# A decode kernel's tail: the last PSUM copy and the output's issue move to ScalarE, and the early zeros with them

## The chip, the cores and the metric

The kernel runs on one core of a Trainium2 chip. A core has five engines that run side by side and meet at semaphores: TensorE (PE, matrix products into PSUM; its weight loads are listed as PEld), VectorE (DVE), ScalarE (ACT), GpSimd (POOL) and SyncE (SP), which here only issues DMAs and waits. DMAs of all issuers run on the core's 16 DMA engines. The metric is the time of one execution on the device in microseconds (us); a profile of one execution gives the single instructions.

## The reference

A decode step of a gated mix of two branches, for a batch of 2 and one token of width 640, all in fp32:

```
g = sigmoid(sum(x * gate_w))
q = (x @ wq) as 32 heads of 128
o = softmax(q . k_cache / sqrt(128)) @ v_cache      # 4096 cached positions per head
a = o (4096 wide) @ wo                              # back to 640
b = silu(x @ w1) @ w2                               # 640 -> 1728 -> 640
out = g * a + (1 - g) * b                           # (2, 1, 640)
```

Nearly all of the work is reading: the two caches are 2 x 32 x 4096 x 128 floats each, 134 MB apiece, and `wq` and `wo` are 10.5 MB each.

## The kernel before, in words

The kernel is written as a list of operations per engine (`Flow`). Each operation names the buffers that it reads and writes; `plan` (line 75) works out from the order in the text which semaphores it must wait for. A write waits for all earlier readers of the same name, and a DMA counts as done once its own semaphore stands at 16. What an engine has already learned through another engine's wait isn't waited for again. Each engine runs its operations strictly in the order of the text.

Three slabs `v`, `b` and `a` of SBUF take the loads, all issued by SP in one order: `w1`, then `x` and the gate, `w2`, `wq` (lines 303 to 312), a DMA of zeros from the cleared buffer `oP` into the output (line 328), and then the caches. There are N = 16 rounds, one for each group of four heads and each row of the batch. A round loads a K part (8.4 MB) and a V part (8.4 MB). DVE and POOL multiply K with the query (lines 670 and 676), DVE sums to scores (686), ACT takes the exponentials (715), PE multiplies them with V (766), and DVE turns the result into columns of `oP` (837). `load_k(i + 2)` waits for the scores of round i, `load_v(i)` for PE's products of round i - 1. Six loads of `wo` follow the last V.

The start: DVE transposes `x` and the gate (line 420), copies `x` into the cleared buffer `xz` (424), works out `x @ w1` (443 to 446), PE the rest of the feed-forward branch (533) and `x @ wq` into two PSUM banks (608). `ps_0` holds heads for u = 0, `ps_1` for u = 1; ACT takes both out into `qall`, once for each row of the batch, four instructions (647). The first K load waits for line 446, since it overwrites `w1`; the first V load waits for line 608.

The end: `in_halves` (556) sums `wo` products for three quarters of the heads into the PSUM bank `early`, `merge` copies that to SBUF on ACT (568) and joins it by matmuls with the sums `acc` in `ps_0` (573), and `in_quarters` (586) adds the last quarter as its pieces of `wo` land. Then DVE copies `acc` to SBUF (891), SP issues the output (892), counts `s_sent` so that POOL may clear the semaphores (904 and 905), and waits for the output to land (897).

`once` (line 123) wraps a stretch of an engine's operations, given by their indices in `spans`, in a loop that runs once, with a hint for fetching code ahead.

## Time and profile before

| | |
|---|---|
| median of 3 runs | 695.96 us |
| lowest and highest | 695.74, 696.21 us |
| the profiled execution | 695.71 us |
| its span, first to last instruction | 694.2 us |
| instructions | 3593 |
| DVE busy | 507.5 us, 73% |
| POOL busy | 265.6 us, 38% |
| PE busy | 211.4 us, 30% |
| ACT busy | 40.0 us, 6% |
| read from HBM | 298.26 MB, 430 GB/s over the span |

A profile row reads: start and length in us (or, for groups, their sum and the mean in ns), engine, line of the kernel, operation, the buffer written and those read, shapes. "SPq" is SP's own instruction stream. In brackets, or behind the bar, stands how long the engine had been idle and what ended that. DMA instructions in such rows are only the issue; the data move later.

### The profile page before, as it was taken

The numbers are of one execution on the slowest core, as the hardware profiler recorded it, in microseconds if no ns is written. First come the engines' busy times: TensorE is split into PE (matmuls) and PEld (weight loads), VectorE is DVE, ScalarE is ACT, GpSimd is POOL, SyncE is SP. The second block draws the span as 40 slices with busy tenths as digits, with TensorE's granted clock in tenths as the row PEclk, the third lists the DMA queues.
The fourth block names the chain that finished last, engine by engine and source line by source line (L and its number), as shares of the span: only waits on it lengthen the run. The fifth ranks groups of instructions, "written<-read, shape, count | busy, mean of one in ns | idle before, by whom it ended". The sixth has DMA issues, their size and how long they took to land. (4 is left out here: it accounts for less than half of the span.)

```text
span 694.2 us, 3593 instructions
## 1 busy us (share of the span) xinstructions
PE 211.4 (30%) x1440; PEld 72.5 (10%) x1440; DVE 507.5 (73%) x269; ACT 40.0 (6%) x152; POOL 265.6 (38%) x26
## 2 busy tenths in 40 slices
PE   0074032151331405060412306060503315050657
PEld 0032010010110101020100101010100101010113
DVE  3810958898989596886959596986959595977811
ACT  0001010101010101010010101010000101010000
POOL 1000808191726090815335180906244270907100
PEclk9998556565565757575665757575655757575689
DMA  9999999999999999999999999999999999999997
GB/s 383 430 446 450 430 427 424 423 457 438 427 430 423 430 461 427 434 423 423 438 457 427 430 423 427 464 430 430 423 423 461 434 430 427 423 438 457 427 408 326
DMA packets 6209, 298.33 MB, mean 430 GB/s; under 512 B 672, under 2 KB 700, under 8 KB 956
## 3 DMA queue, kind: packets, MB, share of 16 engines
q1 hardware_dynamic: 6204, 298.27, 99.4%
q8 instruction: 2, 0.03, 0.0%
q14 instruction: 3, 0.02, 0.0%
HBM read 298.26 MB, written 0.01 MB: 430 GB/s over the span
## 5 line engine op out<-in xcount | busy, mean ns | idle before, releaser
L670 POOL TENSOR_TENSOR slabs<-slabs,qsb 128x7680 f32<-128x7680 f32 x16 | 262.3, 16396 | 378.7 <-DMA slabs<-in_A_k_cache_dram 347.8
L686 DVE TENSOR_REDUCE s<-slabs 128x68 f32<-128x8704 f32 (+1 forms) x32 | 276.3, 8676 | 0.0
L766 PE MATMUL ps<-slabs,pz 128*32 128x512 f32 x1024 | 146.2, 735 | 345.2 <-PEq L145 338.2
L676 DVE TENSOR_TENSOR slabs<-slabs,ps 128x8704 f32<-128x8704 f32 x16 | 147.5, 9218 | 108.5 <-DMA slabs<-in_A_k_cache_dram 108.4
L766 PEld LDWEIGHTS ps<-slabs,pz 128*32 128x32 f32 x1024 | 39.5, 132 | 438.6 <-issue 431.6
L715 ACT ACTIVATE pz<-s,nb 32x128 f32<-32x128 f32 x64 | 25.4, 398 | 556.5 <-PE ps L766 363.2
L804 PE MATMUL ps<-osb,pick 128*128 128x512 f32 x32 | 20.4, 724 | 58.9 <-PEq L145 58.0
L818 DVE TENSOR_REDUCE row<-ps 64x128 f32<-64x512 f32 x16 | 10.9, 682 | 23.3 <-PE ps L804 23.3
L788 DVE SCALAR_TENSOR_TENSOR osb<-ps,rg,own 128x512 f32<-128x512 f32 x16 | 12.0, 748 | 21.4 <-PE ps L766 21.2
L618 PE MATMUL ps<-qall,spread 128*128 (+1 forms) x32 | 7.4, 319 | 35.3 <-PEq L145 34.5
L446 DVE SCALAR_TENSOR_TENSOR slabs<-slabs 128x1728 f32<-128x1728 f32 x8 | 16.1, 2019 | 0.3
L458 PE MATMUL ps<-slabs,xz_col 128*32 128x432 f32 x16 | 3.1, 928 | 33.2 <-DVE slabs L446 33.2
L804 PEld LDWEIGHTS ps<-osb,pick 128*128 128x128 f32 x32 | 5.4, 211 | 73.0 <-issue 71.2
L715 ACT ACTIVATION_READ_ACCUMULATOR pz<-s,nb 32x1 f32 x64 | 11.8, 184 | 0.0
L618 PEld LDWEIGHTS ps<-qall,spread 128*128 128x128 f32 x32 | 6.9, 224 | 44.9 <-issue 43.2
L533 PE MATMUL ps<-slabs,seq 128*32 128x320 f32 x54 | 10.3, 545 | 3.7 <-DVE seq L512 3.7
L825 DVE STREAM_TRANSPOSE ps<-row 64x256 f32<-64x256 f32 x16 | 10.3, 642 | 0.6
L608 PE MATMUL ps<-slabs,xz_col 128*32 128x512 f32 x80 | 9.8, 593 | 0.0
L891 DVE COPY slabs<-ps 128x160 f32<-128x160 f32 x1 | 0.3, 325 | 12.2 <-PE ps L586 12.2
L556 PE MATMUL ps<-slabs,oP_xs 128*32 128x320 f32 x96 | 8.8, 433 | 1.4 <-DMA slabs<-in_A_wo_dram 1.4
L740 PE MATMUL ps<-rs,fold 128*128 128x1 f32 x32 | 6.1, 260 | 2.3 <-PEq L145 2.1
L740 PEld LDWEIGHTS ps<-rs,fold 128*128 128x128 f32 x32 | 5.7, 222 | 5.0 <-issue 3.5
(63 smaller groups left out, 71.9 us busy)
## 6 DMA issues: line engine op xcount, KB each, us to landing
slabs<-in_A_wq_dram SPq DMA_DIRECT2D x1, 10240.0 KB, 44.5
slabs<-in_B_w_dram SPq DMA_DIRECT2D x2, 4320.0 KB, 17.0
slabs<-in_A_wo_dram SPq DMA_DIRECT2D x1, 5120.0 KB, 21.5
slabs<-in_A_wo_dram SPq DMA_DIRECT2D x2, 1280.0 KB, 25.4
slabs<-in_A_wo_dram SPq DMA_DIRECT2D x1, 1600.0 KB, 30.1
slabs<-in_A_wo_dram SPq DMA_DIRECT2D x1, 640.0 KB, 31.1
slabs<-in_A_wo_dram SPq DMA_DIRECT2D x1, 320.0 KB, 31.4
slabs<-in_A_k_cache_dram SPq DMA_DIRECT2D x16, 47.8
```

The lines of the kernel that those rows point to most:

```text
L446: lambda b=b, j=j, at=at: V.scalar_tensor_tensor(hsum[:, b, :], w1t[:, j, :], at, hsum[:, b, :], op0=ALU.mult, op1=ALU.add)
L533: last = T_.matmul(early[to : to + 32, :], seq[:, k : k + 2, :].rearrange("p k z -> p (k z)"), slab[n][:, k * HD : (k + 1) * HD], start=(k ...
L618: return T_.matmul(ps_q[:, :DH], spread, qall.rearrange("p h b d -> p (h b) d")[:, i, :], start=True, stop=True,)
L670: lambda: G_.tensor_mul(k[:, CV:, :], k[:, CV:, :], qsb[:, None, :].to_broadcast([P, C - CV, DH])),
L676: lambda: V.tensor_mul(k[:, :CV, :], k[:, :CV, :], ps_q[:, None, :DH].to_broadcast([P, CV, DH])),
L686: lambda c0=c0, c1=c1: V.reduce_sum(Ss[i % 2][:, c0:c1], k[:, c0:c1, :], axis=AX.X),
L715: last = S_.activation(pz[lo:hi, :, 4 * q : 4 * q + 4], s[lo:hi].rearrange("p (g c) -> p g c", c=4), AF.Exp, bias=nb[lo:hi], scale=SCALE, ...
L740: lambda *_: T_.matmul(ps_t[:, :1], fold.rearrange("p a q c -> p (a q c)"), rs, start=True, stop=True),
L766: last = T_.matmul(ps_v[32 * q : 32 * q + 32, :], pz[:, gr, :], v[:, gr, :], start=(gr < 4), stop=(gr >= NG - 4),)
L788: lambda: V.scalar_tensor_tensor(osb, ps_v.rearrange("p (c d) -> p c d", d=DH), rg, own[:, :, None].to_broadcast([P, 4, DH]), op0=ALU.mult ...
L804: lambda *_: T_.matmul(ps_o, pick, osb.rearrange("p c d -> p (c d)"), start=True, stop=True),
L818: lambda: V.reduce_sum(row, ps_o[:64].rearrange("p (c d) -> p d c", d=DH), axis=AX.X),
```

## The change

Five things change. The last copy out of PSUM (`ot` from `acc`) runs on ACT in place of DVE, and ACT issues the output DMA and counts `s_sent`; SP keeps the wait for the landing. The early DMA of zeros is issued by ACT, from `xz_col` in place of `oP`. The copy in `merge` runs on DVE in place of ACT. The two `qall` copies for u = 1 run on DVE in place of ACT. The stretch of ACT's operations that `once` wraps moves by one index. Since the zeros are now a reader of `xz`, and line 424 writes `xz`, that copy now waits for the zeros' DMA.

```diff
     out_rows = out.rearrange("b s (n d) -> (s n) b d", n=G)
-    f.dma("SP", out_rows, oP[0:P:HB, :W], reads=["oP"], writes=["out"])
+    f.dma("ACT", out_rows, xz_col[0:P:HB, :W], reads=["xz"], writes=["out"])
...
     def merge():
-        f.op("ACT", lambda: S_.copy(partial, early), reads=["ps_acc"], writes=["partial"])
+        f.op("DVE", lambda: V.tensor_copy(partial, early), reads=["ps_acc"], writes=["partial"])
...
     for u in range(2):
         for b in range(B):
+            to = qall[:, u * HALF : (u + 1) * HALF, b, :]
+            src = qr[u].rearrange("p (h d) -> p h d", d=DH)
             f.op(
-                "ACT",
-                lambda u=u, b=b: S_.mul(
-                    qall[:, u * HALF : (u + 1) * HALF, b, :],
-                    qr[u].rearrange("p (h d) -> p h d", d=DH),
-                    mask[:, b : b + 1],
+                ("ACT", "DVE")[u],
+                (
+                    (lambda to=to, src=src, b=b: V.tensor_scalar(to, src, mask[:, b : b + 1], None, op0=ALU.mult))
+                    if u
+                    else (lambda to=to, src=src, b=b: S_.mul(to, src, mask[:, b : b + 1]))
                 ),
...
-    f.op("DVE", lambda: V.tensor_copy(ot, acc), reads=["ps_0"], writes=["ot"])
-    f.dma("SP", out_rows, ot[0:P:HB, :], reads=["ot"], writes=["out"], signal=s_out)
-
-
-    def land():
-        nc.sync.sem_inc(s_sent)
-        return nc.sync.wait_ge(s_out, 16).then_inc(s_out, -16)
-
-    f.op("SP", land).signal = "sent"
+    f.op("ACT", lambda: S_.copy(ot, acc), reads=["ps_0"], writes=["ot"])
+    f.dma("ACT", out_rows, ot[0:P:HB, :], reads=["ot"], writes=["out"], signal=s_out)
+
+
+    f.op("ACT", lambda: S_.sem_inc(s_sent)).signal = "sent"
+    f.op("SP", lambda: nc.sync.wait_ge(s_out, 16).then_inc(s_out, -16)).signal = "sent"
...
-    spans = {"ACT": (14, 34), "DVE": (100, 220), "PE": (len(f.ops["PE"]) - NP * PR - 1, len(f.ops["PE"]))}
+    spans = {"ACT": (15, 35), "DVE": (100, 220), "PE": (len(f.ops["PE"]) - NP * PR - 1, len(f.ops["PE"]))}
```

## The prediction

> **What bounds the kernel now.** The first view is the page's summary: the load on the DMA engines in 40 slices and the queues (packets, MB, share of the engines' time).

> ```profile
> span 694.2 us, 3593 instructions
> ...
> DMA  9999999999999999999999999999999999999997
> ...
> q1 hardware_dynamic: 6204, 298.27, 99.4%
> q8 instruction: 2, 0.03, 0.0%
> q14 instruction: 3, 0.02, 0.0%
> HBM read 298.26 MB, written 0.01 MB: 430 GB/s over the span
> ```

> The reader is to see a full row of nines: the 16 DMA engines work from the first slice to the last but one, and one queue, that of SyncE (SP), holds 99.4% of their time. The end is therefore set by when the 298 MB have come in, plus what follows the last piece of `wo`. An edit can move the time by over 0.2% (1.4 us of 696, about what a measurement of this kernel can tell from no change) only if it starves that queue, or lengthens the tail.

> The tail is in the second view, the chain of work that ended last in order of time (start, length, what), and the third, the instructions of the last microseconds (in brackets: idle time before, and what ended it).

> ```profile
> 659.21 30.07 DMA slabs<-in_A_wo_dram
> 689.28 0.14 issue
> ...
> 691.61 0.51 PE ps L586 x8
> ```
> ```profile
> 686.69 1.51 PE L556 MATMUL ps<-slabs,oP_xs 128*32 128x320 f32 x10
> ...
> 688.25 0.43 ACT L568 COPY slabs<-ps 128x320 f32<-128x320 f32 x1 [28.38 <-PE ps L556]
> ...
> 688.73 0.47 PE L573 MATMUL ps<-slabs,join 128*17 128x160 f32 x8 [0.53 <-ACT slabs L568]
> ...
> 690.87 0.41 PEld L586 LDWEIGHTS ps<-slabs,oP_xs 128*17 128x17 f32 x16 [0.23 <-DMA slabs<-in_A_wo_dram]
> 691.61 0.13 PEld L586 LDWEIGHTS ps<-slabs,oP_xs 128*17 128x17 f32 x8 [0.34 <-DMA slabs<-in_A_wo_dram]
> 692.15 0.33 DVE L891 COPY slabs<-ps 128x160 f32<-128x160 f32 x1 [12.24 <-PE ps L586]
> 692.50 0.58 SPq L69 DMA_DIRECT2D out_dram<-slabs  x1
> ```

> TensorE waits for a piece of `wo` at 689.28, at 690.87 and at 691.61; eight last matmuls end at 692.12; VectorE (DVE) copies until 692.48, SP issues the output from 692.50 to 693.08. The span ends at 694.2, so the output needs 694.2 - 693.08 = 1.12 us from the end of its issue to being waited out. That makes 2.1 us after the last matmul, the only stretch on the path that the change rewrites.

> The fourth view has the beginning: the waits and issues on which the loads hang.

> ```profile
> 2.44 0.27 POOL L323 MEMSET xz_col<- 128x208 f32 x1
> ...
> 2.63 0.56 SPq L69 DMA_DIRECT2D oP_xs<-in_gate_w_dram  x1
> 3.23 0.43 SPq L69 DMA_DIRECT2D slabs<-in_B_w_dram  x1
> 3.71 0.43 SPq L69 DMA_DIRECT2D slabs<-in_A_wq_dram  x1
> ...
> 4.18 0.59 SPq L69 DMA_DIRECT2D out_dram<-oP_xs  x1
> ...
> 13.75 0.46 DVE L420 STREAM_TRANSPOSE slabs<-oP_xs 128x160 f32<-128x160 f32 x1 [7.72 <-DMA oP_xs<-in_gate_w_dram]
> 14.25 0.18 DVE L424 COPY xz_col<-slabs 128x10 f32<-128x10 f32 x1
> ...
> 33.22 0.34 SPq L69 DMA_DIRECT2D slabs<-in_A_k_cache_dram  x1
> ...
> 36.91 0.17 ACT L477 ACTIVATE ge<-ps 128x2 f32<-128x2 f32 x1 [34.90 <-PE ps L473]
> ...
> 59.51 0.33 SPq L69 DMA_DIRECT2D slabs<-in_A_v_cache_dram  x1
> 59.52 2.42 ACT L647 ACTIVATE qall<-ps,mask 128x512 f32<-128x512 f32 x4 [20.28 <-PE ps L608]
> ...
> 61.82 0.28 ACT L640 COPY qsb<-ps 128x128 f32<-128x128 f32 x1
> 68.36 9.22 DVE L676 TENSOR_TENSOR slabs<-slabs,ps 128x8704 f32<-128x8704 f32 x1 [27.86 <-DMA slabs<-in_A_k_cache_dram]
> 68.41 16.39 POOL L670 TENSOR_TENSOR slabs<-slabs,qsb 128x7680 f32<-128x7680 f32 x1 [64.40 <-DMA slabs<-in_A_k_cache_dram]
> ```

> **The change part by part.** Durations of the two copying engines, by shape (busy us, mean ns), and of `wq` to its landing:

> ```profile
> L640 ACT COPY qsb<-ps 128x128 f32<-128x128 f32 x16 | 4.3, 267 | 5.9 <-PE ps L618 5.8
> L568 ACT COPY slabs<-ps 128x320 f32<-128x320 f32 x1 | 0.4, 426 | 28.4 <-PE ps L556 28.4
> L891 DVE COPY slabs<-ps 128x160 f32<-128x160 f32 x1 | 0.3, 325 | 12.2 <-PE ps L586 12.2
> L788 DVE SCALAR_TENSOR_TENSOR osb<-ps,rg,own 128x512 f32<-128x512 f32 x16 | 12.0, 748 | 21.4 <-PE ps L766 21.2
> ```
> ```profile
> slabs<-in_A_wq_dram SPq DMA_DIRECT2D x1, 10240.0 KB, 44.5
> ```

> 1. *Last copy, DVE to ScalarE (ACT).* ACT's slope is (426 - 267) / (320 - 128) = 0.83 ns per column, so 160 columns take 267 + 32 x 0.83 = 293 ns against 325: -0.03 us. ACT began 0.05 us after L556 ended (686.69 + 1.51 = 688.20 to 688.25), DVE 0.03 us after L586: +0.02. Sum -0.01 us, on the path. [...]

> 2. *Output issued by ACT.* The wait that SP had on DVE (692.48 to 692.50) becomes ACT's wait on its own copy: 0.02 us again, by the 0.04 us between the dependent DVE instructions at 13.75 and 14.25. No row shows ACT issuing a DMA; SP's issues run from 0.33 us (the loads) to 0.59 (the zeros). I take 0.58, the output's own row, since rows and bytes are the same; bounds -0.25 and, doubled, +0.58. The landing, 1.12 us: I take no difference, since the same DMA engines are idle by then; bounds are nothing at all (-1.12) and twice that (+1.12, a queue unused for 690 us).

> 3. *The count for the clearing.* `sem_inc(s_sent)` now stands behind ACT's issue, as it stood behind SP's; POOL's clearing waits for it.

> ```profile
> L905 POOLq EVENT_SEMAPHORE_RANGE_CLEAR  x1: 243/243/243, 693.2 to 693.2; - x1
> ```

> It ends by 693.5, 0.7 us ahead of the end: 0. With that cover gone it would cost what it is late. SP has nothing queued but its wait for the landing, as before.

> 4. *Merge copy, ACT to DVE.* DVE has been idle for 12.24 us when it would start. Its price for 320 columns: 325 ns plus 160 columns at 0.89 ns, the slope to the row below, = 467 ns, against 426: +0.04 us.

> ```profile
> L495 DVE COPY spaced<-ps 128x224 f32<-128x224 f32 x2 | 0.7, 382 | 0.0
> ```

> The merging matmuls end at 688.73 + 0.47 = 689.20 and would end at 689.24; the first piece of `wo` comes at 689.28, and TensorE waits for data twice more (0.23 and 0.34 us on its weight loads). Cost 0; without those waits +0.04.

> 5. *Two of the four `qall` products, ACT to DVE.* ACT's four take 2.42 us, two some 1.25. DVE's two, at most 0.75 each by its 512-column row, run from 59.52 to 61.0, while DVE is idle until 68.36. ACT's copy of the first query moves up by about 1.2 us, but POOL, which reads it, waits for K until 68.41. Cost and gain 0; the cover is 7 us, without it +1.5.

> 6. *Early zeros, SP to ACT.* SP loses one issue (4.18, 0.59 us) of a queue then idle until 33.22: 0. ACT waits for POOL's clearing of `xz_col` (2.71), issues 0.6 us, and behind it stands its table load, 1.3 us; needed at 36.91. New: the copy into `xz` (L424, 14.25) now waits until the zeros have been read and written, and all DVE work stands behind it. If ACT's queue is served beside SP's, 5 KB issued at 3.3 are written long before 13.75, when DVE's wait for `gate` ends: 0.

> 7. *Shifted code* (the stretch run once on ACT, indices 15 to 35): a fetch of code there falls into ACT's long waits, such as the 34.90, 20.28 and 28.38 us in the rows above: 0, the tail apart (rival B); without such waits a small transfer, 1.7 us by the output's own issue to landing (692.50 to 694.2).

> Sum against the profiled execution: 695.71 us (1.5 beyond its span), -0.01, so 695.70. The runs' median is 695.96, 0.25 above it: 695.95, say 695.9.

> **The rivals.**

> *A. The zeros come late (slower).* In the kernel before, the zeros stood behind `w2` and `wq`; were DMAs served in order of issue whatever the queue, L424 would wait. Its delay d passes to the K load at 33.22 and over the feed-forward matmuls to the V load at 59.51. `wq` lands at 3.71 + 44.5 = 48.2, 13 us behind K's issue and its 1.7 us to land; K lands at 68.36, so the queue runs dry first from d = 68.36 - 59.51 - 1.7 = 7.2 us, that is if the zeros land after 21.4. Behind `w2` (4320 KB at 430 GB/s after 13.75: 24.0) d is 9.8 and the loss 2.6: 698.5 us. Behind `wq` d is 34: K dry for 48.2 to 68.9, V again for some 7, 723 us. Against it: ACT's issue at 2.75 would stand before `w2` (3.23) even in a common order, d = 0. [...]

> *B. The tail on ACT is slower than on SP.* One mechanism: ACT's last instructions, after 28 us of waiting, are fetched only when needed, or its queue must be woken. The page's q14 and q8 show that code comes by DMA. Price: one more small transfer, 1.7 us, so 697.6, slower by 0.24%; it decides from 1.4 us. Against it: L568, ACT's first after 28.38 us, began 0.05 us after its release. Half such a price (0.6 to 1.1) stays within 0.2%.

> *C. Clearly faster.* The tail can't give it: landing for nothing and the cheapest issue are 1.12 + 0.25 = 1.37 us, 694.6, still -0.2%. It would need the zeros to have held up the K load behind them on SP's queue by that much; then 694.5 or less. Against it, the stretches around that place show no dip in the last column, GB/s:

> ```profile
> 34.00:46.00 12.00, 8.32 (x40) 2.82 (x34) 2.86 (x11) 0.42 (x2) 0.00 (x0) 1.00 1.00 433
> 46.00:48.00 2.00, 2.00 (x18) 0.79 (x14) 0.00 (x0) 0.00 (x0) 0.00 (x0) 1.00 1.36 588
> 48.00:50.00 2.00, 2.00 (x20) 0.91 (x19) 0.00 (x0) 0.00 (x0) 0.00 (x0) 1.00 1.06 459
> ```

> **How the numbers follow.** Forecast, no change that can be told: 0.82. A 0.04 and B 0.10, slower: 0.14. C, faster: 0.04. The range goes from 695.3 (half of the landing saved) to 697.2 (issue +0.15, landing doubled), which holds the forecast and the smaller half of B; A and the rest of B lie above it.

> **What would show it.** In the profile after: ACT's copy of 160 columns near 0.29 us and DVE's of 320 near 0.47, the merging matmuls over before the first `wo` piece; ACT's issue near 0.58 and about 1.1 us from its end to the end of the span; L424's successor still released by `gate` at about 13.75; K still issued near 33.2. Wrong would be a wait of DVE for the zeros, an ACT issue or landing over a microsecond longer, or a DMA row with a hole.

## The result and the profile after

The changed kernel takes 697.9 us, the median of 8 runs, against 695.92 for 8 runs of the kernel before: 1.0031 times as long, 95% interval 1.0022 to 1.004. That is 2.0 us slower, where no change was forecast. Two of the eight executions took 699.42 and 699.54 us, with 4.6 and 4.8 us outside the span in place of 3.2 to 3.3; why is not known.

The profiled execution took 697.61 us. Its span, first to last instruction, is 694.4 us, only 0.2 above that of before. So nearly all of the loss lies outside the span: 697.61 - 694.43 = 3.2 us in place of 695.71 - 694.21 = 1.5. The page's summary, same lines as before:

```profile
span 694.4 us, 3591 instructions
...
DMA  9999999999999999999999999999999999999997
...
q1 hardware_dynamic: 6180, 298.26, 99.3%
q8 instruction: 3, 0.05, 0.0%
q10 hardware_dynamic: 24, 0.01, 0.0%
q14 instruction: 1, 0.01, 0.0%
HBM read 298.26 MB, written 0.01 MB: 430 GB/s over the span
```

The loads run without a hole, as before. ACT's own queue, q10, is new. And q14, of the kind that the page calls "instruction" (code, as it is read here), has one packet inside the span in place of three. The DMA view, cut to stretches around the end and beyond it (packets, MB, share of the engines' time in the stretch), shows where the other two went. First the kernel before, 688 to 694 us:

```profile
q14 instruction: 2, 0.02, 0.6%
```

There are none from 694 on. Then the changed kernel, 694 to 698 us:

```profile
q14 instruction: 2, 0.02, 1.4%
```

The trace's packets on q14 near the end, with ACT's last instruction beside them:

```
                ACT's last        code packets on q14,        last packet   time of the
                instruction ends  8192 bytes each, start      ends          execution
before          688.67            690.27, 692.65              692.96        695.71
changed kernel  693.34            694.44, 696.70              697.24        697.61
```

Two packets of code follow ACT's last instruction. Before, they were over at 692.96, while the output was still under way. Now they end 0.4 us ahead of the end of the execution.

The tail itself, in the order of time:

```profile
688.47 0.49 DVE L568 COPY slabs<-ps 128x320 f32<-128x320 f32 x1 [7.98 <-PE ps L556]
...
689.02 0.47 PE L573 MATMUL ps<-slabs,join 128*17 128x160 f32 x8 [0.59 <-DVE slabs L568]
...
691.08 0.41 PEld L586 LDWEIGHTS ps<-slabs,oP_xs 128*17 128x17 f32 x16 [0.35 <-DMA slabs<-in_A_wo_dram]
691.86 0.13 PEld L586 LDWEIGHTS ps<-slabs,oP_xs 128*17 128x17 f32 x8 [0.38 <-DMA slabs<-in_A_wo_dram]
692.40 0.29 ACT L893 COPY slabs<-ps 128x160 f32<-128x160 f32 x1 [33.63 <-PE ps L586]
692.72 0.57 ACTq L69 DMA_DIRECT2D out_dram<-slabs  x1
```

It is close to what was predicted, row by row: the last weights still wait for `wo`, the copy takes 0.29 us, and the issue 0.57. From the issue's end at 693.29 to 694.41, when SP's wait for the landing ends, pass 1.12 us. Behind the issue ACT counts `s_sent`, its last instruction:

```profile
L897 ACTq EVENT_SEMAPHORE  x1: 17/17/17, 693.3 to 693.3; - x1
```

And the beginning:

```profile
2.73 1.22 ACTq L69 DMA_DIRECT2D out_dram<-xz_col  x1
3.99 1.28 ACT L477 ACT_TABLE_LOAD   x1 [3.99 <-issue]
...
14.30 0.46 DVE L420 STREAM_TRANSPOSE slabs<-oP_xs 128x160 f32<-128x160 f32 x1 [8.27 <-DMA oP_xs<-in_gate_w_dram]
14.79 0.18 DVE L424 COPY xz_col<-slabs 128x10 f32<-128x10 f32 x1
...
33.77 0.34 SPq L69 DMA_DIRECT2D slabs<-in_A_k_cache_dram  x1
...
60.12 0.33 SPq L69 DMA_DIRECT2D slabs<-in_A_v_cache_dram  x1
```

DVE still waits for `gate`, not for the zeros; all of it is 0.55 to 0.6 us later than before, where the prediction's sum for rival A has the load queue 7.2 us in hand.

### The profile page after: what moved, and what is told of

Same layout as the page of the kernel before. It is cut to its first block, busy times and chain, and to the rows that moved or that the text cites. A ratio compares the mean times of both kernels' runs of the same rounds, so it can differ in the third digit from the quotient of the medians.

```text
span 694.4 us, 3591 instructions
## 1 busy us (share of the span) xinstructions
PE 213.9 (31%) x1440; PEld 72.7 (10%) x1440; DVE 509.2 (73%) x271; ACT 38.8 (6%) x150; POOL 265.6 (38%) x26
## 2 busy tenths in 40 slices
DMA  9999999999999999999999999999999999999997
## 3 DMA queue, kind: packets, MB, share of 16 engines
q1 hardware_dynamic: 6180, 298.26, 99.3%
HBM read 298.26 MB, written 0.01 MB: 430 GB/s over the span
## 5 line engine op out<-in xcount | busy, mean ns | idle before, releaser
L768 PE MATMUL ps<-slabs,pz 128*32 128x512 f32 x1024 | 148.6, 745 | 342.5 <-PEq L145 334.2
L618 PE MATMUL ps<-qall,spread 128*128 (+1 forms) x32 | 7.4, 319 | 35.0 <-PEq L145 34.2
L650 DVE TENSOR_SCALAR qall<-ps,mask 128x512 f32<-128x512 f32 x2 | 1.4, 747 | 19.4 <-PE ps L608 19.4
L618 PEld LDWEIGHTS ps<-qall,spread 128*128 128x128 f32 x32 | 6.8, 224 | 44.7 <-issue 43.0
L608 PE MATMUL ps<-slabs,xz_col 128*32 128x512 f32 x80 | 9.8, 593 | 0.0
L556 PE MATMUL ps<-slabs,oP_xs 128*32 128x320 f32 x96 | 8.8, 433 | 1.0 <-DMA slabs<-in_A_wo_dram 1.0
L420 DVE STREAM_TRANSPOSE slabs<-oP_xs 128x160 f32<-128x160 f32 x1 | 0.5, 459 | 8.3 <-DMA oP_xs<-in_gate_w_dram 8.3
## 6 DMA issues: line engine op xcount, KB each, us to landing
slabs<-in_A_wq_dram SPq DMA_DIRECT2D x1, 10240.0 KB, 44.7
```

What stands on the lines that cost most here:

```text
L556: last = T_.matmul(early[to + 32 * n : to + 32 * n + 32, :], oP[:, at : at + 32], slab["v"][:, s_ * D + n * W2 : s_ * D + (n + 1) * W2], s ...
L618: return T_.matmul(ps_q[:, :DH], spread, qall.rearrange("p h b d -> p (h b) d")[:, i, :], start=True, stop=True,)
L768: last = T_.matmul(ps_v[32 * q : 32 * q + 32, :], pz[:, gr, :], v[:, gr, :], start=(gr < 4), stop=(gr >= NG - 4),)
```

## Experiments: what is it that follows ACT

Theory 1: the way out of the program takes ACT some 4 us after its last instruction, with two fetches of code; it was hidden as long as ACT ended at 688.7. Rival 2: an output on ACT's own queue, or any second queue, costs time outside the span. Rival 3: ACT and DVE have a few instructions more or fewer, and their code is fetched at other places. In what follows "beyond" is the time less the span, as a median over the runs (ten where nothing else is said); it is 1.37 us for the kernel before, timed again beside each group of runs. Some executions have about 1 us more beyond than the rest of their kernel (for the kernel before, 2 of the 31 beside the first group and 3 of the 19 beside the last). Nothing here explains them; they are named where several of a kernel's ten are of that sort.

**ACT held to the end, in the kernel before.** Nothing moves; ACT only waits for DVE's last copy.

```diff
     f.op("SP", land).signal = "sent"
+    f.op("ACT", lambda: S_.sem_inc(s_sent), reads=["ot"]).signal = "sent"
...
-        G_.wait_ge(s_sent, 1).then_inc(s_sent, -1)
+        G_.wait_ge(s_sent, 2).then_inc(s_sent, -2)
```

> The kernel before, with one thing added: ACT waits at the very end for DVE's last copy and counts s_sent too (POOL's clearing waits for two counts). Theory 1 (an engine's way out of the program takes ACT some 4 us more, in which code is fetched; it is hidden as long as ACT's last operation comes at 688, and shows when it comes at 693): the span stays at 694.2, the time goes to about 697.0, 2.8 beyond the span in place of 1.5. Rival 2 (the output on ACT's own DMA queue, or a second DMA queue in use, costs time outside the span): no DMA of ACT here, so 695.9. Rival 3 (the shifted code of ACT and DVE: other places of fetches): one or two instructions more on ACT alone, 695.9.

Measured: 696.86 us, 1.0016 times before (1.0006 to 1.0025); beyond 1.92. ACT's last instruction ends at 692.8:

```profile
L900 ACTq EVENT_SEMAPHORE  x1: 17/17/17, 692.8 to 692.8; - x1
```

Its two code packets start at 693.75 and 695.87, and the profiled execution took 696.78. So part of the loss comes without any DMA of ACT's, against rival 2. Theory 1 had the time about right (697.0) and the split wrong: 2.8 beyond a span of 694.2 was expected, and the span of the profiled execution is 694.93, which no run explains. What the late ACT adds beyond the span is 0.55 us.

**SP issues the output, in the changed kernel.** ACT keeps the last copy and the zeros.

```diff
-    f.dma("ACT", out_rows, ot[0:P:HB, :], reads=["ot"], writes=["out"], signal=s_out)
+    f.dma("SP", out_rows, ot[0:P:HB, :], reads=["ot"], writes=["out"], signal=s_out)
...
-    f.op("ACT", lambda: S_.sem_inc(s_sent)).signal = "sent"
+    f.op("SP", lambda: nc.sync.sem_inc(s_sent)).signal = "sent"
```

> The changed kernel, with SP issuing the output and counting s_sent as in the kernel before; ACT still makes the last copy and still sends the zeros. Theory 1: ACT is done 0.65 us earlier (692.7 in place of 693.3), so 697.2, 2.6 beyond the span. Rival 2 in the form that the output on ACT's queue is what costs: 695.9, 1.5 beyond the span. Rival 2 in the form that any second queue costs: 697.9.

Measured: 696.71 us, 1.0015 (1.0005 to 1.0025); beyond 2.0, with six executions at 1.85 to 2.0 and four at 2.6 to 3.2. ACT ends at 692.90 and the code packets start at 693.62 and 695.87. The medians gain about 1.2 us on the changed kernel, the two profiled executions 0.83 (697.61 and 696.78). Of that, ACT's earlier end is 0.44, and the first fetch came 0.4 us sooner after it. Theory 1 had put the time at 697.2, so its direction holds and its size is off by 0.5. Rival 2 isn't settled by this run: the time fell with the output's move to SP, though not to 695.9.

**The old tail, in the changed kernel.** Merge copy on ACT, last copy on DVE, output on SP; zeros on ACT, split `qall` and the shifted loop stay.

```diff
-        f.op("DVE", lambda: V.tensor_copy(partial, early), reads=["ps_acc"], writes=["partial"])
+        f.op("ACT", lambda: S_.copy(partial, early), reads=["ps_acc"], writes=["partial"])
...
-    f.op("ACT", lambda: S_.copy(ot, acc), reads=["ps_0"], writes=["ot"])
-    f.dma("ACT", out_rows, ot[0:P:HB, :], reads=["ot"], writes=["out"], signal=s_out)
+    f.op("DVE", lambda: V.tensor_copy(ot, acc), reads=["ps_0"], writes=["ot"])
+    f.dma("SP", out_rows, ot[0:P:HB, :], reads=["ot"], writes=["out"], signal=s_out)
...
-    f.op("ACT", lambda: S_.sem_inc(s_sent)).signal = "sent"
+    f.op("SP", lambda: nc.sync.sem_inc(s_sent)).signal = "sent"
```

> The changed kernel, with the tail of the kernel before: merge copied on ACT, last copy on DVE, output issued by SP. The zeros on ACT's queue, the split of qall and the shifted run-once stretch stay. Theory 1: ACT's last operation is back at 688.5, so 695.9 to 696.1, 1.5 beyond the span. Rival 2 (any second queue costs): 697.9. Rival 3 (shifted code): 697.9.

Measured: 695.87 us, 0.9997 (0.9987 to 1.0007); beyond 1.37. ACT ends at 688.82, the packets are back at 690.08 and 692.22. The zeros on a second queue, the split of `qall` and the moved loop together cost nothing that can be measured. Rival 2 is out in the form that any second queue costs, and rival 3 as a cost by itself. That the output on ACT's queue costs is not refuted here, since SP issues it; that falls two runs below.

**ACT waits for the landing, in the changed kernel.** The wait moves from SP to ACT, which then ends last of all.

```diff
-    f.op("SP", lambda: nc.sync.wait_ge(s_out, 16).then_inc(s_out, -16)).signal = "sent"
+    f.op("ACT", lambda: S_.wait_ge(s_out, 16).then_inc(s_out, -16)).signal = "sent"
```

> The changed kernel, with ACT in place of SP waiting for the output to land, so that ACT's last operation comes at 694.4 in place of 693.3 and the span stays. Theory 1 (what follows ACT's last operation sets the time: two fetches of code, some 4.3 us from the last operation to the end): the time grows with ACT's end by 1.1 us, to 698.7 to 699.0. If the loss were a fixed cost of ACT's queue or of the launch, 697.6 to 697.9 stays.

Measured: 698.8 us, 1.0044 (1.0027 to 1.006), 4 runs; beyond 4.2. That is what theory 1 had. ACT's last instruction, and q14 from 694 to 698 us:

```profile
L898 ACTq EVENT_SEMAPHORE  x1: 17/17/17, 694.2 to 694.2; - x1
```
```profile
q14 instruction: 2, 0.02, 1.3%
```

The four profiled executions so far in which ACT ends late have nearly the same sum, from ACT's end to the end of the time: 696.78 - 692.79 = 4.0, 696.78 - 692.90 = 3.9, 697.61 - 693.34 = 4.3, 698.33 - 694.25 = 4.1 us. Before, 688.67 + 4.1 = 692.8 was well ahead of the rest.

## Experiments: why ACT's way out needs two fetches

**No run-once loop on ACT, in the changed kernel.** The same operations in a straight line.

```diff
-    spans = {"ACT": (15, 35), "DVE": (100, 220), "PE": (len(f.ops["PE"]) - NP * PR - 1, len(f.ops["PE"]))}
+    spans = {"ACT": (-1, -1), "DVE": (100, 220), "PE": (len(f.ops["PE"]) - NP * PR - 1, len(f.ops["PE"]))}
```

> The changed kernel without the run-once loop on ACT (its operations stand in one straight line; DVE and PE keep theirs). If ACT's late fetches follow from where its code lies and from the jump of that loop, the time beyond the span changes, to 1.5 (time 695.9) or upwards; if they come with the end of any program on ACT, theory 1 in its plainest form, 697.9 stays. Rivals 2 and 3 have no reason for a change: 697.9.

Measured: 695.78 us, 0.9998 (0.9988 to 1.0007); beyond 1.35. The whole loss is gone, though ACT still ends at 693.25. Theory 1 in its plainest form, that any late end of ACT costs 4 us, falls with it. So does what was left of rival 2, for the output is still on ACT's queue. The DMA view of this kernel has a code packet from 228 to 248 us:

```profile
q1 hardware_dynamic: 144, 8.39, 96.9%
q14 instruction: 1, 0.01, 0.1%
```

The changed kernel has none there:

```profile
q1 hardware_dynamic: 154, 9.04, 104.3%
```

At the end (694 to 698 us) one packet is left, at 694.79, and the time is no longer than that of the kernel before (0.9998):

```profile
q14 instruction: 1, 0.01, 0.5%
```

The packet at 236.13 follows a copy of ACT (the first row below, from this run). In the changed kernel the loop on ACT runs from its hint at 170.9 to its branch at 427.1 (the other two rows), over just that place.

```profile
234.57 0.27 ACT L640 COPY qsb<-ps 128x128 f32<-128x128 f32 x1
```
```profile
L132 ACTq BRANCH_PREFETCH_HINT  x1: 55/55/55, 170.9 to 170.9; - x1
```
```profile
L135 ACTq COMPARE_BRANCH  x1: 67/67/67, 427.1 to 427.1; - x1
```

Theory 1a, then: ACT's code comes in pieces of 8192 bytes. Crossing into one piece starts the fetch of the one after it. If the crossing happens inside the loop, that fetch is not made, and ACT makes up for it at its end, where it must wait. Rival, 1b: any loop on ACT has the effect, by its jump or its extra instructions. The next two runs move the loop off the place.

**The loop ends before the place, or begins behind it.**

```diff
-    spans = {"ACT": (15, 35), "DVE": (100, 220), "PE": (len(f.ops["PE"]) - NP * PR - 1, len(f.ops["PE"]))}
+    spans = {"ACT": (15, 18), "DVE": (100, 220), "PE": (len(f.ops["PE"]) - NP * PR - 1, len(f.ops["PE"]))}
```

> The changed kernel, with the run-once loop on ACT shortened to operations 15 to 17 (171 to about 204 us). Without the loop ACT fetched code at 236 us, behind the copy at 234.6. Theory 1a (a loop that spans that place keeps the fetch from being made there, and it is made up for at the end): this loop ends before it, so a fetch near 236, one fetch at the end, 695.8. Theory 1b (any loop on ACT has that effect, or its few instructions more shift the code): two fetches at the end, 697.6.

```diff
-    spans = {"ACT": (15, 35), "DVE": (100, 220), "PE": (len(f.ops["PE"]) - NP * PR - 1, len(f.ops["PE"]))}
+    spans = {"ACT": (27, 35), "DVE": (100, 220), "PE": (len(f.ops["PE"]) - NP * PR - 1, len(f.ops["PE"]))}
```

> The changed kernel, with the run-once loop on ACT at operations 27 to 34, that is from about 300 to 427 us, behind the place of the fetch at 236. Theory 1a: a fetch near 236, one at the end, 695.8. Theory 1b: two fetches at the end, 697.6.

Measured: 695.91 us, 1.0 (0.999 to 1.001), and 695.87 us, 1.0005 (0.9995 to 1.0015); beyond 1.37 in both (three of the late loop's ten have 2.0 to 2.9). The early loop's branch comes at 203.4, the late loop's hint at 311.9:

```profile
L135 ACTq COMPARE_BRANCH  x1: 67/67/67, 203.4 to 203.4; - x1
```
```profile
L132 ACTq BRANCH_PREFETCH_HINT  x1: 55/55/55, 311.9 to 311.9; - x1
```

Code packets start at 238.24 and 694.33, and at 235.86 and 694.59. From 228 to 248 us, the early and then the late loop:

```profile
q14 instruction: 1, 0.01, 0.1%
```
```profile
q14 instruction: 1, 0.01, 0.1%
```

Both loops add the same instructions of their own as the one that costs 2 us (189 of ACT's are recorded in all three). 1b is out.

**The place moves off the loop.** The loop covers the same operations; 30 small copies more on ACT at the start shift the crossing.

```diff
     f.op("DVE", lambda: V.memset(ones, 1.0), writes=["ones"])
+    pad = sb("pad", [P, 32])
+
+    def more():
+        for k in range(30):
+            last = S_.copy(pad[:, k : k + 1], ones[:, :1])
+        return last
+
+    f.op("ACT", more, reads=["ones"], writes=["pad"])
...
-    spans = {"ACT": (15, 35), "DVE": (100, 220), "PE": (len(f.ops["PE"]) - NP * PR - 1, len(f.ops["PE"]))}
+    spans = {"ACT": (16, 36), "DVE": (100, 220), "PE": (len(f.ops["PE"]) - NP * PR - 1, len(f.ops["PE"]))}
```

> The changed kernel with its run-once loop over the same operations, and 30 one-column copies more on ACT at the start, in its idle time before 36 us. Theory 1a (a loop that spans the place where ACT crosses from one piece of its code to the next keeps the next piece from being fetched): 30 instructions earlier is three rounds earlier, so the crossing moves from 235 to about 135 us, ahead of the loop that begins at 171; a fetch near 136, a second one some 128 instructions later near 580, none or a harmless one at the end, 695.8 to 696.0. If the loop as such, or ACT's late end as such, costs the 2 us: 697.6 to 697.9.

Measured: 695.95 us, 1.0 (0.999 to 1.0009); beyond 1.69, which is the middle of two groups: five executions at 1.3 to 1.4, the profiled one among them, and five at 1.9 to 2.4. In the profiled one code packets start at 170.57 and 584.06, and there is none at the end. The DMA view from 160 to 180, from 574 to 594, and from 688 to 698 us:

```profile
q1 hardware_dynamic: 144, 8.39, 96.8%
q14 instruction: 1, 0.01, 0.1%
```
```profile
q1 hardware_dynamic: 149, 8.72, 100.6%
q14 instruction: 1, 0.01, 0.1%
```
```profile
q1 hardware_dynamic: 283, 0.97, 23.8%
q10 hardware_dynamic: 12, 0.01, 0.2%
```

The second packet is where it was expected. The first came one round later than the 136 us of the expectation, just ahead of the loop's hint at 170.8; why so late is open. This kernel has more code than the one that loses 2 us, and the same loop. Since half of its executions have up to 1 us more beyond the span, and none of those was profiled, the run supports theory 1a by its trace and only in part by its time.

**ACT held to the end, in the kernel before, without its loop.**

```diff
-    spans = {"ACT": (14, 34), "DVE": (100, 220), "PE": (len(f.ops["PE"]) - NP * PR - 1, len(f.ops["PE"]))}
+    spans = {"ACT": (-1, -1), "DVE": (100, 220), "PE": (len(f.ops["PE"]) - NP * PR - 1, len(f.ops["PE"]))}
```

The rest is as in the first experiment.

> The kernel before with ACT held to the end, as in the run that gave 696.9, but without ACT's run-once loop. Theory 1a: a fetch near 236, one after ACT's end that nothing waits for, so 695.8 to 696.1, 1.3 to 1.5 beyond the span. If it is ACT's late end alone: 696.9.

Measured: 695.87 us, 1.0003 (0.9993 to 1.0012); beyond 1.46, with a packet at 237.83 and one at 694.12. It takes both: a loop over the crossing (the kernel before has it, from 166.3 to 388.4 us) and an ACT that ends late. Over all the traces but that of the 30 copies more, none of the six kernels whose loop on ACT covers 235 us has a q14 packet there; the five whose loop ends before, begins behind or is absent have one between 235.8 and 238.3. With or without it, three packets come on q14 from the start of the span to the end of the time in the changed kernel and in the one without ACT's loop: the packet near 236 is replaced by a second one at the end.

**No run-once loop at all, in the changed kernel.**

```diff
-    spans = {"ACT": (15, 35), "DVE": (100, 220), "PE": (len(f.ops["PE"]) - NP * PR - 1, len(f.ops["PE"]))}
+    spans = {"ACT": (-1, -1), "DVE": (-1, -1), "PE": (-1, -1)}
```

> The changed kernel without the run-once loops of ACT, DVE and PE. Theory 1: ACT as without its own loop alone, one fetch at its end; the time is 695.8 unless DVE's or PE's code is then fetched at a worse place, in which case the span or what lies beyond it grows by a fetch, 1 to 2 us. A theory in which the loops as such cost time would give less than 695.8.

Measured: 696.23 us, 1.0002 (0.9993 to 1.0012); beyond 1.33, the span 694.9 against 694.3 with the loops of DVE and PE. The difference of 0.45 us to the run without ACT's loop alone is near what can be told here. Its code packets start at 237.87 and 401.23 us, and none is recorded after ACT's end, where the expectation had one; that stays open. From 391 to 411 us:

```profile
q14 instruction: 1, 0.01, 0.1%
```

No other trace has a packet near 401. It lies within DVE's loop (220.5 to 546.0 us in the changed kernel), so the same may hold of DVE, though nothing at DVE's end makes up for it in the other traces: the late fetch is shown for ACT alone. In the profile of this run the `wo` pieces land 0.8 us later than before (690.09 for the one that came at 689.28), and a fetch of 16 KB on q8 at 685.41 lies in that stretch; that the one causes the other was not tested. In four of the traces with PE's loop (677.5 to 692.0 us in the changed kernel) such a fetch comes at 692.9 to 693.4, after PE's last matmul; in two of the four, those of the late loop and of the kernel before with ACT held and no loop on ACT, nothing is lost.

No version beats the kernel before by more than the measurement can tell. The changed kernel without ACT's loop (695.78) is as fast as it.

## Why the prediction was wrong

**The step that failed is the first term of the sum, "695.71 us (1.5 beyond its span)", carried over as if fixed.** Steps 1 to 3 move ACT's last instruction from 688.67 to 693.34, and what still follows that instruction was put at nothing; no line of the prediction asked for it. Some 4 us follow it in this kernel (4.3 in the profiled execution), and the part beyond the span was 3.2. Step 7 is where it should have come up. It set the run-once stretch at 0, because a fetch there would fall into ACT's long waits. For moving the stretch by one index that 0 held: the old-tail run has the moved stretch and loses nothing, and the first experiment has the old stretch and loses time. But the reason speaks only of fetches that are made. What counted is one that is not made there, by the old stretch no more than by the new (neither trace has a q14 packet from 228 to 248 us), and comes after ACT's end (two packets there in the changed kernel, at 694.44 and 696.70, one without ACT's loop, at 694.79). The sign was in the trace of before: the page counts three packets on q14, two of which lie after ACT's last instruction (690.27 and 692.65, the stretch from 688 to 694 above).

**Rival B** had the engine, the kind of cause and about the size (fetched code on ACT, 1.7 us, 697.6), with a chance of 0.10. That its size came so near is in part luck: it priced one transfer, and the runs show two, 2.1 to 2.3 us apart, while the first 1.1 of the 4.3 us after ACT's end ran beside the landing of the output (to 694.41). Its place was wrong: it looked between ACT's copy and the landing, where every row came out as forecast. Its argument against itself, that L568 began 0.05 us after its release, says nothing of code that lies behind the last instruction.

**Rival A** is refuted: L420 was released by `gate` at 14.30, and L424 followed at 14.79. The zeros' eight packets started between 6.82 and 9.15 us on q10, beside the load of `w1`, each followed within 0.04 us by a packet of q1. So the two queues were served side by side here, which step 6 had as an "if". **C** did not happen: q1 gave up its 24 packets, but the K load was issued no earlier (33.77 us), and the loads kept 430 GB/s.

Step by step: step 1, ACT's copy, forecast 293 ns, measured 292, right. Step 2, issue 0.58 and landing 1.12, measured 0.57 and 1.12, right. Step 3, the clearing, 243 ns from 693.46, still ahead of 694.4, right. Step 4, DVE's copy forecast 467 ns, measured 491. It began 0.2 us later than ACT's had, and the merging matmuls ended at 689.49 in place of 689.24; the first piece of `wo` came at 689.47 here, so nothing was left in hand, and the two later waits for `wo` covered it. (The 12.24 us for which step 4 has DVE idle are its wait up to the last copy; up to the merge copy it was idle for 7.98. That changes nothing in the sum.) Step 5, DVE's two `qall` rows 747 ns each, right, hidden. Step 6: the zeros' issue took 1.22 us in place of 0.6, and `gate` came 0.55 us later; both were covered, and the old-tail run puts steps 5, 6 and the moved loop together at no measurable cost.

The range (to 697.2) missed because its upper end was built from the issue and the landing alone.

## What to carry to other kernels

The span is not the time: 3.2 us of the changed kernel's lay outside it. In it the code packet that five other versions had near 236 us did not come, two came after ACT's last instruction, and the time ended 4.3 us after that. So before the last work is moved to another engine, look at that engine's end, at code packets behind it, and at what lies between time and span. A loop should be checked in the same way when a code packet shows in its place once it is taken out. Ending it before that place, beginning it behind, or leaving it out cost nothing here and gave the 2 us back.
